# Chunked attention, gated convolution and two projections on one core: another written-out order, which places GpSimd's pieces beside VectorE pieces that read PSUM or one operand

## The chip, the cores and the metric

One core of a Trainium2 chip runs the whole kernel as one program. The metric is device time in microseconds (us), as the median of several runs; smaller is better. The engines are TensorE (PE in the profile, its weight loads PEld), VectorE (DVE), ScalarE (ACT), GpSimd (POOL) and SyncE (SP), which issues the DMAs here.

## What is computed

Attention within chunks of 64 positions, for 8 batches, 8 heads, 576 positions and 64 values per head, and behind it a block in which a causal convolution of five taps makes a gate for a projection. Inputs and outputs are 32-bit floats.

```python
scores = scale * np.matmul(q_c, k_c.transpose(0, 1, 2, 4, 3))
attn = np.exp(scores - np.max(scores, axis=-1, keepdims=True))
attn = attn / (np.sum(attn, axis=-1, keepdims=True) + 1e-09)
x = np.matmul(attn, v_c)            # heads side by side: batch x 576 x 512
for k in range(K):                  # K = 5, zeros ahead of each batch
    gate_pre += conv_w[k] * xp[:, k:k + S, :]
out = (1 / (1 + np.exp(-gate_pre)) * (x @ w_val)) @ w_out
```

## The kernel before, in words

The 8 x 576 positions are cut into nine stages g = 0 to 8 of 512 positions each. The features lie on the partitions, 128 at a time, so a stage has four feature blocks and two pairs of them, p = 0 and 1.

The order of all work is written out by hand, or by a planner, in the string `ORDER`. It is a list of short pieces; the loop at the end of the function calls one Python function for each, in that order, and `tc.keep_in_program_order` keeps it. Every engine works through its own pieces strictly in that order, and waits where a piece needs the result of another engine or a buffer that is still in use. Which buffer a piece gets is written out too, in `SLOTS`: one digit for each allocation of a name.

The pieces, with the engine that does each:

- `lq`, `lk`, `lv g p`: loads of queries, keys and values (SyncE; tiles `qt`, `kt`, `vt`, two buffers each). `lw n c`: block c of the weights of `x @ w_val` (n = v) or of the output projection (n = o); `lc`: the tap weights. The raw weights go into `acc` buffers. `st g t`: store of an output tile `o`.
- `w1` to `w9`, `wa`, `wb`: each weight block arrives as raw bits and is split into a high part (`v_hi`, `o_hi`) and a low part (`v_lo`, `o_lo`). `w1`, `w3`, `w4`, `w7` are VectorE's, `w2`, `w5`, `w6` ScalarE's, `w8`, `wa`, `wb` GpSimd's; with a D behind the name (`waD`) VectorE does the piece.
- Attention of a pair: `S g p b` (score products into PSUM tile `s`, 32 recorded products each), `mx` (row maximum), `sb` (subtract it, into `e_row`), `ex` (exponential, ScalarE), `sm` (row sum `rs` and its reciprocal), `nm` (normalise, tile `en`; GpSimd, or VectorE as `nmD`), `T` (eight transposes into `et`), `ec` (copy to `eb`, ScalarE), `A` (products with the values, into two `ps` banks of PSUM).
- The projection's input: `xr` (rounded copy `xh`, ScalarE), `xd` (the rest, `xl`, VectorE, which reads PSUM), `xc` (plain copy `x` for the convolution), `hl` (the four positions ahead of a stage, GpSimd).
- Convolution of feature block h: `k0` (first tap, ScalarE, or VectorE as `k0D`), `k g h j` (taps j = 1 to 4, VectorE, SCALAR_TENSOR_TENSOR on `acc`), `sg` (sigmoid, ScalarE).
- Value projection: `V g m c`, three products of 512 columns (`xh` with `v_hi`, `xh` with `v_lo`, `xl` with `v_hi`) added into one of four `ps` banks over c = 0 to 3; `gm g m` multiplies that bank by the gate (VectorE, tile `gt`) and frees it.
- Output projection: `gr` (rounded copy `gh`, ScalarE), `gd` (the rest, `gl`, GpSimd, or VectorE as `gdD`), `P g t c` (three products again, into a `ps` bank), `oc` (copy to `o`, ScalarE, or VectorE as `ocD`).
- `W n`: n products of a zero tile `warm`, whose result is used by nobody. `zr`, `zi`, `zw` set constants.

Pieces of several stages stand mixed. At the start the four `v` and four `o` weight blocks are split between the softmax work of the first pairs and the first taps, all largely on VectorE. The four `ps` banks serve `A`, `V`, `P` and `W` in turn, so a `V` or `P` piece with c = 0 waits until VectorE or ScalarE has read the bank's last contents.

A line number of the profile is of little use here, since every instruction is recorded on the one line of `run`; the tile names tell the pieces apart.

Of the kernel before, what the change touches and what calls it, by code (L numbers as in the profile page):

```python
# [514 lines left out]
```

## Time and profile before

| | |
|---|---|
| median of 3 runs | 305.24 us (304.71 to 305.42) |
| the profiled execution's own time | 305.96 us |
| its span, first to last instruction | 304.2 us |
| TensorE busy / VectorE busy | 274.9 us / 266.1 us |
| ScalarE busy / GpSimd busy | 185.2 us / 85.5 us |
| moved by DMA | 42.47 MB |

Busy time is the union of an engine's instructions, waits inside them included: a VectorE instruction that is held by another engine counts as busy and shows a longer duration. Products are pipelined, so a product's own duration (0.40 us) is longer than the distance from one start to the next. The timeline merges neighbours of one kind, with their count behind x.

### The profile page before, as it was taken

To read this page: it belongs to the slowest core of one execution; us is meant where nothing else is said; L and a number is where in the kernel's file an instruction comes from. 1 tells how busy PE (TensorE), PEld (TensorE's weight loads), DVE (VectorE), ACT (ScalarE), POOL (GpSimd) and SP (SyncE) were. 2 spreads that over 40 slices of the span, in tenths; PEclk is the share of its full clock that TensorE was granted. 3 is DMA by queue.
4 is the path that set the end of the run, shared out by engine and by line. 5 is a ranking of instruction groups with operands and counts; after the bars stand their busy time and mean duration, and the time that the engine had idled before them with its cause. 6 is when DMAs were issued, how large, how long until landed. Compare 5 with 4: busy or idle time off the path is not lost.

```text
span 304.2 us, 7897 instructions
## 1 busy us (share of the span) xinstructions
PE 274.9 (90%) x3356; PEld 218.4 (72%) x3361; DVE 266.1 (87%) x374; ACT 185.2 (61%) x314; POOL 85.5 (28%) x77
## 2 busy tenths in 40 slices
PE   0688663989999999999899989999999999999995
PEld 0456442768887888888777877887888888788883
DVE  4799999989999999999999999979998877679710
ACT  4268656676678796885816976465567825732401
POOL 1535740424155026106430541063200600100100
PEclk9999996999999999999999999999999999999999
DMA  6997403601481752362662732124250014211013
GB/s 239 414 404 246 155 2 125 214 11 43 166 284 65 276 183 102 105 224 91 209 237 110 236 113 71 69 90 155 102 213 36 1 45 124 78 71 50 19 76 132
DMA packets 14291, 42.47 MB, mean 140 GB/s; under 512 B 1712, under 2 KB 1712, under 8 KB 14256
## 3 DMA queue, kind: packets, MB, share of 16 engines
q1 hardware_dynamic: 14256, 41.97, 38.6%
q8 instruction: 26, 0.43, 0.6%
q14 instruction: 9, 0.07, 0.1%
HBM read 32.53 MB, written 9.44 MB: 138 GB/s over the span
## 4 chain that ended last, share of the span: by engine, by line
PE 57%; DVE 31%; DMA 5%; issue 4%; SPq 1%; ACT 1%; DVEq 0%; ACTq 0%
PE ps L160 50%; DVE acc L160 12%; PE s L160 4%; DVE gt L160 4%; DVE e_row L160 4%; DVE rs L160 3%; DVE mx L160 3%; DVE xl L160 2%; DMA kt<-in_k 2%; PE et L160 2%; DMA vt<-in_v 2%; DVE gate L160 1%; SPq L160 1%; DVE gl L160 0%; DVE v_lo L160 0%
## 5 line engine op out<-in xcount | busy, mean ns | idle before, releaser
L160 DVE SCALAR_TENSOR_TENSOR acc<-x,cw,acc 128x516 f32<-128x516 f32 (+1 forms) x144 | 113.1, 818 | 2.9 <-ACT acc L160 1.8
L160 POOL TENSOR_TENSOR gl<-gt,gh 128x512 fp32r<-128x512 f32 x24 | 32.7, 1365 | 149.5 <-ACT gh L160 149.5
L160 PE MATMUL ps<-xh,v_hi 128*128 128x512 f32 x144 | 59.5, 413 | 6.2 <-DVE xl L160 6.2
L160 PE MATMUL ps<-xl,v_hi 128*128 128x512 f32 x144 | 57.3, 398 | 3.1 <-DVE xl L160 3.1
L160 PE MATMUL ps<-o_hi,gh 128*128 128x512 f32 x144 | 58.4, 405 | 0.0
L160 PE MATMUL ps<-xh,v_lo 128*128 128x512 f32 x144 | 57.2, 397 | 0.0
L160 PE MATMUL ps<-o_lo,gh 128*128 128x512 f32 x144 | 56.9, 395 | 0.0
L160 PE MATMUL ps<-o_hi,gl 128*128 128x512 f32 x144 | 56.9, 395 | 0.0
L160 ACT ACTIVATE gate<-acc 128x512 f32<-128x512 uint32 (+8 forms) x72 | 30.3, 466 | 20.9 <-DVE acc L160 20.7
L160 POOL TENSOR_TENSOR en<-e_row,rs 128x1024 f32<-128x1024 f32 x16 | 32.4, 2022 | 23.0 <-DVE rs L160 22.5
L160 PEld LDWEIGHTS ps<-xh,v_hi 128*128 128x128 f32 x144 | 27.2, 189 | 13.1 <-DVE xl L160 6.6
L160 ACT COPY o<-ps 128x512 f32<-128x512 f32 x27 | 15.7, 584 | 32.1 <-PE ps L160 30.3
L160 PEld LDWEIGHTS ps<-xl,v_hi 128*128 128x128 f32 x144 | 27.2, 189 | 10.4 <-DVE xl L160 3.9
L160 PE MATMUL s<-kt,qt 64*64 64x64 f32 x1152 | 23.5, 231 | 12.3 <-DMA kt<-in_k 10.1
L160 PEld LDWEIGHTS s<-kt,qt 64*64 64x64 f32 x1152 | 20.8, 144 | 17.1 <-issue 15.5
L160 PEld LDWEIGHTS ps<-o_hi,gl 128*128 128x128 f32 x144 | 27.1, 188 | 6.5
L160 PEld LDWEIGHTS ps<-o_hi,gh 128*128 128x128 f32 x144 | 27.1, 188 | 6.5 <-issue 0.2
L160 PEld LDWEIGHTS ps<-xh,v_lo 128*128 128x128 f32 x144 | 27.4, 190 | 5.5
L160 PEld LDWEIGHTS ps<-o_lo,gh 128*128 128x128 f32 x144 | 27.1, 188 | 5.8
L160 ACT CAST gh<-gt 128x512 fp32r<-128x512 f32 x36 | 22.1, 618 | 13.7 <-DVE gt L160 13.5
L160 ACT ACTIVATE e_row<-e_row 128x1024 f32<-128x1024 f32 x18 | 19.1, 1061 | 17.8 <-DVE e_row L160 17.7
L160 ACT CAST xh<-ps 128x512 fp32r<-128x512 f32 x36 | 20.8, 592 | 14.8 <-PE ps L160 14.3
(56 smaller groups left out, 373.6 us busy)
## 6 DMA issues: line engine op xcount, KB each, us to landing
qt<-in_q SPq DMA_DIRECT2D x18, 512.0 KB, 4.9
kt<-in_k SPq DMA_DIRECT2D x18, 512.0 KB, 6.4
vt<-in_v SPq DMA_DIRECT2D x18, 512.0 KB, 4.5
out<-o SPq DMA_DIRECT2D x36, 256.0 KB, 2.3
acc<-in_moe_w_val SPq DMA_DIRECT2D x4, 512.0 KB, 6.3
acc<-in_moe_w_out SPq DMA_DIRECT2D x4, 512.0 KB, 9.0
raw_cw<-in_moe_conv_w SPq DMA_DIRECT2D x1, 20.0 KB, 1.7
```

The costliest lines, as they stand in the source:

```text
L160: return tc.keep_in_program_order(fn(*args, **kwargs))
```

## The change

`ORDER` and the strings of `SLOTS` that go with it are replaced as a whole; no function, no shape and no tile size differs. What the new list has otherwise than the old one, counted piece by piece:

- the same computation, but other engines for some pieces: four more `gd` on VectorE (16 for 12), two more `nm` on VectorE (4 for 2), two more `oc` on VectorE (11 for 9), one `xc` fewer on VectorE (4 for 5); four first taps fewer on VectorE (1 for 5); of the weight pieces `wb v 1`, `wb v 2`, `wb o 0`, `wb o 3`, `wa o 0` and `w8 o 3` go from VectorE to GpSimd, and `wa v 0`, `wa v 2` and `w8 o 2` from GpSimd to VectorE;
- 87 warm products in eight pieces `W` for 49 in six; `W 8` and `W 16` now stand ahead of the first score products;
- everything else in another order, on all engines and on SyncE's queue.

```diff
--- before.py
+++ after.py
-ORDER = """zw,zr 1,lc,hl 0,zi,lw v 1,zr 0,lw v 0,lq 0 0,lk 0 0,lw v 2,lw v 3,w3 c 0,w1 c 0,lk 0 1,w2 c 0,w5 c 0,w4 c 0,lq 0 1,
-w7 c 0,w8D c 0,w9,w1 v 1,w3 v 1,w2 v 1,w5 v 1,w1 v 0,w4 v 1,lw o 2,w2 v 0,lv 0 0,w3 v 0,w5 v 0,w7 v 1,w6 v 1,w4 v 0,
-lw o 0,w8D v 1,w6 v 0,S 0 0 0,w7 v 0,S 0 0 1,waD v 1,W 14,w8 v 0,mx 0 0,lq 1 0,lk 1 0,wa v 0,sb 0 0,w3 v 2,ex 0 0,
-w3 v 3,wbD v 1,w5 v 2,w1 v 2,S 0 1 0,sm 0 0,wb v 0,S 0 1 1,W 10,lk 1 1,w1 v 3,lv 0 1,mx 0 1,nm 0 0,w2 v 3,lq 1 1,
...
+ORDER = """zw,hl 0,lc,zi,lw v 1,W 8,zr 1,zr 0,lw v 0,lq 0 0,lk 0 0,lw v 2,lk 0 1,w1 c 0,w3 c 0,w2 c 0,lw v 3,w5 c 0,w4 c 0,
+w7 c 0,lq 0 1,W 16,w1 v 1,w3 v 1,w2 v 1,w8D c 0,w9,w1 v 0,w5 v 0,w4 v 1,w2 v 0,w3 v 0,w5 v 1,w7 v 1,w6 v 1,w4 v 0,
+w8D v 1,w6 v 0,S 0 0 0,w7 v 0,S 0 0 1,waD v 1,W 14,w8 v 0,w5 v 2,mx 0 0,lk 1 0,lw o 2,lq 1 1,wb v 1,sb 0 0,w1 v 2,
+ex 0 0,w1 v 3,w3 v 2,waD v 0,w2 v 2,S 0 1 0,w2 v 3,sm 0 0,wb v 0,S 0 1 1,w5 v 3,W 9,lq 1 0,mx 0 1,lv 0 0,nm 0 0,
+lw o 0,lk 1 1,sb 0 1,lv 1 0,T 0 0,w4 v 2,ex 0 1,W 7,w3 v 3,w7 v 2,w6 v 2,sm 0 1,w8 v 2,ec 0 0,A 0 0,w4 v 3,nmD 0 1,
+S 1 0 0,xr 0 0 0,lv 0 1,S 1 0 1,w7 v 3,xc 0 0 1,lw o 1,T 0 1,w1 o 0,xc 0 0 0,lk 2 0,waD v 2,w5 o 0,W 11,mx 1 0,
+wb v 2,w2 o 0,ec 0 1,xd 0 0 0,w8 v 3,k0 0 0,sb 1 0,w3 o 0,ex 1 0,S 1 1 0,k 0 0 1,lw o 3,S 1 1 1,lq 2 0,w4 o 0,
...
-    acc="01230132130213021302132013",
-    qt="010101101000110010",
-    kt="010101010010101110",
-    gate="0123450123450134343013250413250143201543021534201543",
-    gt="01010101101010101010010110100110101101011001",
-    vt="010101010101101001",
+    acc="01231032013201320132013210",
+    qt="010110100001001101",
+    kt="010101010100010101",
+    gate="0123450312450312451403241503241053241032451023405123",
+    gt="01010110100110101010101010011001101010101010",
+    vt="010010110100001010",
...
```

Three places, as the built programs have them. First GpSimd, from `nm 1 0` on (tile `en`; `gate`, `o_hi` and `o_lo` belong to weight pieces `w8`, `wa`, `wb`; `gl` to `gd`). Before:

```order
L160 TENSOR_TENSOR en_543<-e_row_63,rs_439 128x1024
L160 TENSOR_TENSOR gate_522<-gate_522,gate_346 128x512
L160 TENSOR_TENSOR en_575<-e_row_64,rs_547 128x1024
L160 TENSOR_TENSOR gate_633<-gate_633,gate_626 128x512
L160 TENSOR_TENSOR gate_626<-gt_623,o_hi 128x512
L160 TENSOR_TENSOR gl_795<-gt_753,gh_755 128x512
```

and now:

```order
L160 TENSOR_TENSOR en_569<-e_row_63,rs_550 128x1024
L160 TENSOR_TENSOR gate_407<-gt_439,o_hi 128x512
L160 TENSOR_TENSOR o_lo<-gate_407,gate_413 128x512
L160 TENSOR_TENSOR en_633<-e_row_64,rs_578 128x1024
L160 TENSOR_TENSOR gate_649<-gate_649,gate_612 128x512
L160 TENSOR_TENSOR gate_612<-gt_731,o_hi 128x512
```

Before, `nm 1 0` and `nm 1 1` have one weight piece (`w8 o 2`) between them; now two, `wa o 0` and `wb o 0`.

VectorE at the same place, from the row sum of pair 1 1 on (`acc<-x,cw,acc` is a tap; `gt<-acc`, `gate<-acc`, `gt<-gate,gt` and `gate<-gt` are `w3`, `w1`, `w4` and `w7`). Before:

```order
L160 TENSOR_REDUCE rs_547<-e_row_64 128x16
L160 RECIPROCAL rs_547<-rs_547 128x16
L160 SCALAR_TENSOR_TENSOR acc_545<-x_74,cw,acc_545 128x512
L160 SCALAR_TENSOR_TENSOR acc_437<-x_74,cw,acc_437 128x512 x2
L160 SCALAR_TENSOR_TENSOR acc_545<-x_74,cw,acc_545 128x512
L160 TENSOR_TENSOR gate_348<-gt_406,o_hi 128x512
L160 SCALAR_TENSOR_TENSOR acc_437<-x_74,cw,acc_437 128x512 x2
L160 TENSOR_SCALAR gt_623<-acc_397 128x512
```

and now:

```order
L160 TENSOR_REDUCE rs_578<-e_row_64 128x16
L160 RECIPROCAL rs_578<-rs_578 128x16
L160 SCALAR_TENSOR_TENSOR acc_436<-x_71,cw,acc_436 128x512
L160 TENSOR_SCALAR gt_593<-acc_211 128x512
L160 TENSOR_SCALAR gate_612<-acc_396 128x512
L160 SCALAR_TENSOR_TENSOR gt_593<-gate_518,gt_593 128x512
L160 SCALAR_TENSOR_TENSOR acc_436<-x_71,cw,acc_436 128x512
L160 TENSOR_SCALAR gate_518<-gt_593 128x512
L160 SCALAR_TENSOR_TENSOR acc_436<-x_71,cw,acc_436 128x512 x2
```

Before, five taps and the two steps `waD` and, later, `wbD` of block o 0 follow the row sum; now one tap, then `w3 o 2`, `w1 o 1` and `w4 o 2`, and the other taps behind them.

SyncE's queue, where the last loads of the first stages stand (`acc<-in_moe_w_out` is `lw o`, and the first `vt` is `lv 1 1`). Before:

```order
L160 DMA acc_397<-in_moe_w_out 128x1024
L160 DMA qt_464<-in_q 128x1024
L160 DMA acc_637<-in_moe_w_out 128x1024
L160 DMA kt_641<-in_k 128x1024
L160 DMA qt_691<-in_q 128x1024
L160 DMA kt_694<-in_k 128x1024
L160 DMA vt_705<-in_v 128x1024
```

and now:

```order
L160 DMA acc_460<-in_moe_w_out 128x1024
L160 DMA qt_478<-in_q 128x1024
L160 DMA kt_516<-in_k 128x1024
L160 DMA vt_545<-in_v 128x1024
L160 DMA qt_548<-in_q 128x1024
L160 DMA qt_641<-in_q 128x1024
L160 DMA qt_875<-in_q 128x1024
```

Before, `lv 1 1` is behind `lq 3 0` and `lk 3 0`, which need the buffers of `lq 2 0` and `lk 2 0`; now it is ahead of `lq 2 1`, `lq 4 1` and `lq 3 0`.

## Rows read from the trace of the kernel before

**Rows 1.** The page's first part: engine, busy us (share of the span), instructions.
```profile
PE 274.9 (90%) x3356; PEld 218.4 (72%) x3361; DVE 266.1 (87%) x374; ACT 185.2 (61%) x314; POOL 85.5 (28%) x77
```

**Rows 2.** Chain that ended last, in order of time: start us, us, what.
```profile
9.94 2.02 PE s L160 x64
...
55.45 6.58 DMA vt<-in_v
...
233.46 0.93 PE s L160 x64
...
258.66 41.89 PE ps L160 x238
```

**Rows 3.** Timeline of TensorE: start us, us, engine, line, operation, out<-in, count, [idle before].
```profile
12.27 3.50 PE L160 MATMUL ps<-warm 128*128 128x512 bf16 x13 [0.33 <-issue]
...
50.38 0.79 PE L160 MATMUL ps<-xh,v_hi 128*128 128x512 f32 x1 [6.20 <-DVE xl L160]
...
56.44 0.39 PE L160 MATMUL ps<-xh,v_hi 128*128 128x512 f32 x1
...
58.53 0.39 PE L160 MATMUL ps<-xh,v_hi 128*128 128x512 f32 x1
...
62.17 1.16 PE L160 MATMUL ps<-eb,vt 64*64 64x64 f32 x64 [1.38 <-DMA vt<-in_v]
...
176.13 0.69 PE L160 MATMUL s<-kt,qt 64*64 64x64 f32 x32 [1.08 <-DVE acc L160]
```

**Rows 4.** Windows: stretch, its us, PE, PEld, DVE, ACT, POOL busy, PEclk, DMA.
```profile
60.00:70.00 10.00, 8.62 (x154) 6.49 (x153) 8.98 (x14) 7.62 (x14) 2.50 (x2) 1.00 0.06 21
...
90.00:100.00 10.00, 9.77 (x161) 7.84 (x160) 9.96 (x14) 8.20 (x14) 4.62 (x5) 1.00 0.26 102
...
140.00:150.00 10.00, 9.22 (x163) 7.56 (x162) 9.93 (x13) 8.10 (x13) 5.05 (x4) 1.00 0.45 146
...
160.00:170.00 10.00, 9.56 (x169) 7.79 (x168) 9.86 (x14) 7.80 (x14) 2.45 (x2) 1.00 0.25 84
170.00:180.00 10.00, 8.92 (x160) 7.25 (x159) 9.97 (x13) 8.20 (x17) 3.06 (x3) 1.00 0.68 230
```

**Rows 5.** Timeline of GpSimd.
```profile
26.60 2.50 POOL L160 TENSOR_TENSOR gate<-gt,v_hi 128x512 f32<-128x512 f32 x2
32.44 1.32 POOL L160 TENSOR_TENSOR gate<-gate,gate 128x512 f32<-128x512 f32 x1 [3.34 <-DVE gate L160]
...
40.49 2.17 POOL L160 TENSOR_TENSOR en<-e_row,rs 128x1024 f32<-128x1024 f32 x1 [0.77 <-DVE rs L160]
```

**Rows 6.** Timeline of VectorE.
```profile
28.00 1.38 DVE L160 TENSOR_SCALAR gt<-acc 128x512 uint32<-128x512 uint32 x1
...
32.21 0.41 DVE L160 TENSOR_SCALAR gt<-acc 128x512 uint32<-128x512 uint32 x1
...
33.14 1.22 DVE L160 TENSOR_REDUCE mx<-s 128x16 f32<-128x1024 f32 x1
34.27 1.29 DVE L160 SCALAR_TENSOR_TENSOR gt<-gate,gt 128x512 uint32<-128x512 uint32 x1
...
40.24 4.29 DVE L160 SCALAR_TENSOR_TENSOR acc<-x,cw,acc 128x512 f32<-128x512 f32 x4
...
54.43 1.77 DVE L160 SCALAR_TENSOR_TENSOR acc<-x,cw,acc 128x512 f32<-128x512 f32 x1
56.13 0.68 DVE L160 TENSOR_TENSOR gt<-ps,gate 128x512 f32<-128x512 f32 x1
56.73 1.21 DVE L160 TENSOR_REDUCE mx<-s 128x16 f32<-128x1024 f32 x1
...
74.63 6.75 DVE L160 SCALAR_TENSOR_TENSOR acc<-x,cw,acc 128x516 f32<-128x516 f32 x10
```

**Rows 7.** Windows again, one of one microsecond.
```profile
48.00:49.00 1.00, 0.00 (x0) 0.00 (x0) 1.00 (x3) 1.00 (x3) 0.00 (x0) 0.50 0.00 0
```

More of the change, by code (lines that the diff above doesn't have):

```diff
@@ new lines @@
+k0 2 1,k 1 3 4,V 1 2 3,gr 1 1,xd 2 0 0,T 2 1,sg 1 3,gd 1 1,gm 1 2,V 1 3 2,xd 2 0 1,gr 1 2,V 1 3 3,sb 3 0,ec 2 1,
+gd 1 2,P 1 3 0,P 1 3 1,gm 1 3,k 2 1 1,P 1 3 2,ex 3 0,k 2 1 2,A 2 1,k 2 0 1,gr 1 3,S 3 1 0,xc 2 1 0,sm 3 0,gd 1 3,
+S 3 1 1,xr 2 1 0,P 1 0 0,lk 5 1,xr 2 1 1,lq 4 0,P 1 0 1,mx 3 1,nm 3 0,xc 2 1 1,lv 3 1,P 1 3 3,k0 2 2,xd 2 1 0,
+P 1 0 2,oc 1 3,sb 3 1,hl 3,P 1 0 3,k0 2 3,T 3 0,xd 2 1 1,ex 3 1,k 2 1 3,V 2 3 0,ec 3 0,k 2 3 1,V 2 3 1,k 2 0 2,
+V 2 3 2,oc 1 0,k 2 3 2,st 1 0,V 2 3 3,k 2 1 4,A 3 0,k 2 3 3,S 4 0 0,k 2 0 3,xr 3 0 0,S 4 0 1,xr 3 0 1,k 2 0 4,
@@ new lines @@
+P 3 0 3,k 4 1 4,P 3 1 0,k 4 3 1,P 3 1 1,sg 4 1,k 4 3 2,V 4 0 0,oc 3 0,k 4 3 3,st 3 0,V 4 0 1,k 4 3 4,V 4 0 2,
+k 4 2 3,sg 4 3,V 4 0 3,k 4 2 4,P 3 1 2,k 4 0 4,P 3 1 3,gm 4 3,sg 4 0,S 6 1 0,sm 6 0,oc 3 1,A 5 1,S 6 1 1,gm 4 0,
+xr 5 1 0,lv 5 0,nm 6 0,V 4 2 0,mx 6 1,lk 7 1,gr 4 0,V 4 2 1,lq 7 1,xr 5 1 1,st 3 1,V 4 2 2,xc 5 1 0,sb 6 1,gd 4 0,
+ec 5 0,V 4 2 3,xcD 5 1 1,V 4 1 0,gr 4 3,xd 5 1 0,sg 4 2,V 4 1 1,gd 4 3,xd 5 1 1,k0 5 2,V 4 1 2,gm 4 2,A 5 0,k0D 5 3,
+k 5 3 1,S 7 0 0,ex 6 1,lv 6 1,V 4 1 3,k 5 3 2,xr 5 0 0,T 6 0,k 5 3 3,xr 5 0 1,P 2 2 0,gm 4 1,ec 6 0,P 2 2 1,
@@ new lines @@
+k 5 1 2,V 5 1 0,k 6 0 2,oc 2 0,gm 5 0,V 5 2 0,sg 5 2,k 5 1 3,V 5 2 1,gr 5 0,k 5 1 4,A 6 1,sm 7 0,gd 5 0,sg 5 1,
+S 7 1 0,S 7 1 1,gr 5 3,xc 6 1 0,V 5 2 2,gd 5 3,mx 7 1,lq 8 0,xc 6 1 1,lv 7 0,V 5 1 1,st 4 0,V 5 1 2,hl 7,sb 7 1,
+lk 8 1,xr 6 1 0,nm 7 0,V 5 1 3,lv 7 1,xr 6 1 1,xd 6 1 0,V 5 2 3,k0 6 2,xd 6 1 1,P 4 2 0,k0 6 3,gm 5 1,P 4 1 0,
+gm 5 2,T 7 0,k 6 3 1,P 4 2 1,ex 7 1,P 4 2 2,ec 7 0,sm 7 1,P 4 2 3,gr 5 2,A 7 0,ocD 4 2,gd 5 2,S 8 1 0,st 4 2,
+xc 7 0 0,xcD 7 0 1,S 8 1 1,gr 5 1,V 6 3 0,xr 7 0 0,gd 5 1,V 6 3 1,xr 7 0 1,xd 7 0 0,V 6 3 2,k0 7 0,xd 7 0 1,nm 7 1,
@@ new lines @@
+hl 8,P 6 3 1,xr 7 1 0,P 6 3 2,oc 4 1,xd 7 1 0,P 6 3 3,xr 7 1 1,st 4 1,k0 7 3,V 7 3 0,xd 7 1 1,V 7 3 1,sb 8 0,
+V 7 3 2,k 7 0 2,ex 8 0,V 7 3 3,k 7 1 3,P 5 1 0,ex 8 1,k 7 1 4,P 5 1 1,k 7 0 3,P 5 1 2,k 7 0 4,P 5 1 3,k 7 3 1,
+P 5 0 0,oc 5 1,sm 8 0,P 5 0 1,st 5 1,P 5 0 2,V 7 0 0,nmD 8 0,sg 7 0,V 7 0 1,oc 6 3,k 7 3 2,V 7 0 2,st 6 3,lv 8 0,
+k 7 3 3,V 7 0 3,P 5 0 3,k 7 3 4,V 7 2 0,gm 7 0,ocD 5 0,V 7 2 1,gr 7 0,k 7 2 1,sg 7 3,V 7 2 2,gdD 7 0,sg 7 1,V 7 2 3,
+k 7 2 2,T 8 0,k 7 2 3,P 6 0 0,ec 8 0,k 7 2 4,P 6 0 1,gm 7 3,sg 7 2,P 6 0 2,P 6 0 3,gm 7 2,A 8 0,sm 8 1,gr 7 2,
@@ new lines @@
+sg 8 0,k 8 3 2,sg 8 2,P 6 1 2,k 8 3 3,P 6 1 3,V 8 0 3,k 8 3 4,oc 6 1,V 8 1 3,sg 8 3,st 6 1,gm 8 0,V 8 2 0,gm 8 1,
+gr 8 0,V 8 2 1,gdD 8 0,gr 8 1,V 8 2 2,gdD 8 1,V 8 2 3,gm 8 3,P 8 3 0,gm 8 2,gr 8 3,P 7 0 0,gr 8 2,P 7 0 1,gdD 8 2,
+P 8 3 1,gdD 8 3,P 8 3 2,P 8 3 3,P 8 0 0,ocD 8 3,P 8 0 1,st 8 3,P 8 0 2,P 7 1 0,P 7 0 2,P 7 0 3,P 8 1 0,oc 7 0,
+P 7 1 1,st 7 0,P 7 1 2,P 8 2 0,P 7 1 3,P 8 1 1,oc 7 1,P 8 2 1,st 7 1,P 8 2 2,P 8 2 3,P 8 0 3,ocD 8 2,P 8 1 2,st 8 2,
+ocD 8 0,P 7 2 0,st 8 0,P 8 1 3,P 7 2 1,P 7 2 2,ocD 8 1,P 7 2 3,st 8 1,oc 7 2,st 7 2"""
@@ L96 @@
 SLOTS = dict(
     x="010101010",
-    acc="01230132130213021302132013",
-    qt="010101101000110010",
-    kt="010101010010101110",
-    gate="0123450123450134343013250413250143201543021534201543",
-    gt="01010101101010101010010110100110101101011001",
-    vt="010101010101101001",
+    acc="01231032013201320132013210",
+    ps="012320122300211321301320123012310213023201320320120102132012031203120323021320201321312321302123"
+       "21032310231003120310",
+    qt="010110100001001101",
+    kt="010101010100010101",
@@ L114 @@
     xl="012012012012021021",
-    gh="012345670132456745671032567402316745",
-    gl="012345670123456745671023564703214765",
-    o="010110111110100110000110111001011010",
+    gh="012345670231456745670312467502136574",
+    gl="012345670132456745670321476501237564",
+    o="010110001001111010111010100101010101",
 )
```

120 lines of the change are left out of this document (45 added, 75 removed).

## Prediction

> **What bounds the kernel now.** Read the engine table first [rows 1]: TensorE is busy for 274.9 us of 304.2 and VectorE for 266.1. Neither is far from full, so the table does not say which of them sets the end; the chain that ended last does, followed backwards [rows 2]. Its last 41.89 us, from 258.66 us on, are nothing but TensorE, 238 instructions without a gap; behind them stand one copy and one store. Two older pieces of it matter as much: the first score products at 9.94 us, which wait for the first keys, and the wait for a load of values that was issued at 55.45 us. The rest up to 176 us alternates between VectorE and TensorE.
>
> Next look at how TensorE runs once it has work [rows 3]. From 56.44 to 58.53 us it starts nine 512-column products, 0.232 us each, so a piece of three takes 0.70 us. At 50.38 us it starts again after 6.20 us of idling for VectorE's `xl`. **The end is therefore the restart near 50 us, plus the work still left, plus the waits after it.** The ten-microsecond windows give those later waits as what TensorE's busy time lacks of 10.00 [rows 4]: 1.38 + 0.23 + 0.78 + 0.44 + 1.08 = 3.9 us, and every other such window from 70 us on is full up to 300 us. Before the restart the idle time is larger but it belongs to the first 50 us, where VectorE prepares weights, does the softmax of the first pairs and the first taps, and is never idle for long.
>
> Last, what GpSimd does to VectorE [rows 5, 6]. A weight step of 0.41 us (at 32.21) takes 1.38 us at 28.00, beside the second of two GpSimd subtractions (26.60, 2.50 us for two); four taps from 40.24 us take 4.29 us, beside `en` at 40.49; ten free taps in a row take 6.75 us, 0.675 each. The maximum at 33.14 us, which reads PSUM alone, takes 1.22 us although GpSimd works on `gate` from 32.44 us, and the one at 56.73, 1.21 us.
>
> **The change, part by part.**
>
> *Earlier warm matmuls.* W 8 and W 16 now run while the first keys are still on their way. At 9.94 us the first 64 score products take 2.02 us; the same 64 take 0.93 us at 233.46 us [rows 2]. If TensorE is at its higher level by then, VectorE's first maximum starts 1.0 us sooner. The 24 extra matmuls cost at most 24 x 0.27 = 6.5 us (13 recorded in 3.50 us at 12.27, slow ones among them [rows 3]), inside the 9.94 us of waiting, hence nothing. If they all went at half the rate of a 512-column product, 2 x 0.232 x 24 = 11.1 us, the scores would start up to 2 us late but run fast, net 1 us later than now. I take -1.0, since the 3.50 us row is the same instruction; ends -1.1 and +1.0.
>
> *VectorE's queue up to the first gate product (`gm 0 0`, 56.13 us).* The order shows 62 instructions from the first maximum to it before and 60 now. Gone from this stretch: one tap (0.675), one `xd`, `wb v 1`, `wb v 2`, `wa o 0`, `wb o 0`; new in it: `wa v 0`, `wa v 2`, `w8 o 2`, `wb o 2`. At 0.60 us for each two-input step (the start of one at 56.13 to the next start, 56.73 [rows 6]) this is -0.675 - 5 x 0.60 + 4 x 0.60 = **-1.3 us**.
>
> *Contention in that stretch.* Before: 1.38 - 0.41 = 0.97 (28.00), 1.29 - 0.68 = 0.61 (34.27, less a two-input step of the same size, 56.13), 4.29 - 2.70 = 1.59 (40.24, less four free taps), 1.70 - 0.675 = 1.03 (54.43 to the next start); together **4.2 us**. Now: GpSimd's `w8`, `wa`, `wb` of the value weights fall beside maxima, row sums, `xd` and score subtractions, as the change says, and cost nothing there (33.14). But its queue then holds `en`, `wa o 0`, `wb o 0` and `en` of the next pair in a row, and VectorE's holds, after the row sum of pair 1 1, a tap, `w3 o 2`, `w1 o 1`, `w4 o 2`. Laid end to end with the durations above, `wa o 0` ends 0.3 us after that tap wants to start; then a 1.25 us piece stands in front of `w3 o 2` and a 1.9 us piece (2.17 at 40.49, less its own wait) in front of `w1 o 1`. I estimate 0.3 + 1.0 + 1.9 = **3.2 us**, so the change does not clear this stretch. Ends: 0, if the three pieces slip under the row sum, and 0.3 + 1.25 x 2 + 1.9 + 2 x 1.25 = 7.2, if `w8 o 1` and `wa o 1` also land on taps.
>
> What no row here shows is `w1` (one input, two steps apart in memory) beside a GpSimd piece; `w3`, its neighbour, was held (28.00). The Trainium skill's page "SBUF — State Buffer", section "Who interferes with whom", says that GpSimd and a VectorE instruction with two SBUF inputs, or one in a two-port mode, exclude each other for a whole instruction. By that `w1 o 1` waits in full; if it ran free, `w4 o 2` behind it would wait instead and the stretch would be 0.3 us shorter.
>
> So `gm 0 0` starts at 56.13 - 1.0 - 1.3 - 4.2 + 3.2 = 52.8 us and ends 0.68 us later. In the new order it is what frees the PSUM bank for TensorE's next piece, `V 0 2 0`: restart at **53.5 us, 3.1 us later** than 50.38.
>
> *Work done by then.* Before the restart TensorE has finished seven `V` pieces of stage 0; now eight, also the score products of pair 2 0 (0.93) and the transposes of pair 1 1, eight of 128 columns, which by their columns are two products, 0.5, and with switching up to 0.9 (estimate from rows 3). 0.70 + 0.93 + 0.8 = **-2.4 us** of remaining work. TensorE idles about as long as now before the restart (some 7 us against 6.20), so its clock falls as it does at 48 us, where the granted clock is 0.50, the 1.2 GHz level [rows 7], and the slow first products cost the same.
>
> *Waits after the restart.* 1.38 us at 62.17 is the load of `vt` issued at 55.45, because it stood on SyncE behind two loads that wait for score products of pair 2 0; it now stands ahead of them and lands long before its use: gone. 1.08 us at 176.13 [rows 3] is put down to a tap, but scores need no tap; keys for that pair are a likelier cause, and they are now issued farther ahead. The remaining 1.45 us are VectorE being late. With the new order I laid VectorE's running sum (queue and steps of 0.60, 0.675 and, for maxima and the like, 1.13 us, 33.14 to 34.27) against TensorE's 0.70 us pieces: VectorE is 0 to 1 us ahead from 53 to 62 us and 4 to 6 us ahead from 95 to 130 us. Then 2 to 3 us of new contention would still be covered. I keep 1.0 us of waits for chances such as a late `eb` copy or an output slot: **-3.9 + 1.0 = -2.9 us**; ends -3.9 and 0.
>
> *The rest.* VectorE gets four more `gl` and two more `en` (4 x 0.60 + 2 x 1.13) and gives four first taps to ScalarE: about +1 us in all with the copies, all after 56 us, covered by the lead above; without it, 1 us. The other 14 extra warm matmuls (W 18 instead of W 13 and so on) stand where TensorE waits for `xl`; uncovered they would cost 0.22 us each. `vt` and one weight load now stand on SyncE behind a query load that waits for the scores of pair 0 1; they land about 1 us before their use: 0, at worst +1.
>
> **Sum:** +3.1 - 2.4 - 2.9 = **-2.2 us** on the span of 304.2, so 302.0. The profiled execution took 305.96 us, the median of the runs is 305.24; taken off the median, **303.0 us**.
>
> **Rivals.**
>
> 1. *GpSimd's three pieces slip past.* If the `en`, `wa o 0`, `wb o 0` run sits under the row sum and one `xd` more, its 3.2 us fall to about 0.7. For it: the chain in front of them hangs on one ScalarE copy that may come sooner. Against it: `en` alone takes 1.9. Price -2.5 more: 300.5 us.
>
> 2. *The change does not do what it says after the restart.* The contention merely moves, VectorE stays the bound up to 176 us, and of the 3.9 us only the 1.38 us of the load goes; the 1 us more that VectorE gets is then uncovered. The sum is +3.1 - 2.4 - 1.4 + 1.0 = +0.3: 305.5 us, no change that can be told. For it: VectorE lacks less than 0.2 us in every window of rows 4 but the first, and the new order gives it more to do. Against: its lead above.
>
> 3. *The weight stretch gets worse.* All five GpSimd pieces from `wa o 0` to `wa o 1` stand in front of two-input or weight steps, 7.2 instead of 3.2 us: restart at 57.5 us, sum +1.8, 307 us. It decides when `gm 0 0` starts later than 52.8 + 2.2 + 0.6 = 55.6 us. For it: at 40.24 and 54.43 exactly such neighbours were caught, and GpSimd's queue has no pause there now. Against: `w8 o 1` and `wa o 1` have a gate product, `xd` and a maximum beside them. The Trainium skill's page "SBUF — State Buffer", in the same section, says that whichever of the two starts first keeps the shared port for its whole instruction, which speaks for this rival; the tap at 54.43, held for 1.03 us, agrees.
>
> **How the numbers follow.** Forecast 0.46, rival 1 0.20, rival 2 0.17, rival 3 0.17. A measurement of this kernel can tell about 0.2%, 0.6 us, from no change: faster is below 304.6. The forecast and rival 1 lie there, with small parts at their edge: faster 0.66, same 0.17, slower 0.17. The range takes the forecast's own ends, most of rival 1 and of rival 2: 299.8 to 306.0 us; left out are the best of rival 1 and the worst of rival 3.
>
> **What would show it.** Right: the first 64 score products take about 1 us; `gm 0 0` starts between 52 and 54 us; TensorE's wait for `vt` near 62 us is gone; its windows from 60 us on lack about 1 us in all; taps and weight steps of over 1 us stand between 36 and 42 us and hardly elsewhere. Wrong: `gm 0 0` after 55.6 us, or TensorE windows after 60 us that still lack 3 us or more, or the slow score products at the start still there.

## The result, and the profile after

The changed kernel takes **301.84 us** (301.51 to 301.96) against 304.98 for the kernel before in the same series: ratio 0.9887, 95% interval 0.9856 to 0.9919, 3.1 us less. The forecast was 303.0 us, 2.2 us less, with a range of 299.8 to 306.0. The profiled execution took 301.91 us with a span of 300.0.

Against [rows 1] TensorE is now busy 7 us longer in a shorter span (24 more warm matmuls ahead of the first scores are most of it), VectorE 8 us less, with one instruction fewer. The first part of the page:

```profile
PE 282.0 (94%) x3394; PEld 222.1 (74%) x3399; DVE 258.1 (86%) x373; ACT 187.1 (62%) x318; POOL 77.0 (26%) x74
```

TensorE's timeline, to be held against [rows 3]: the first scores, the restart, and the attention product that had waited for the load of values. The first line is the scores before, in the same view; the others are now.

```profile
9.94 1.99 PE L160 MATMUL s<-kt,qt 64*64 64x64 f32 x64 [9.94 <-DMA kt<-in_k]
...
9.55 1.16 PE L160 MATMUL s<-kt,qt 64*64 64x64 f32 x64 [1.54 <-DMA kt<-in_k]
...
53.12 0.79 PE L160 MATMUL ps<-xh,v_hi 128*128 128x512 f32 x1 [6.89 <-DVE gt L160]
60.09 1.16 PE L160 MATMUL ps<-eb,vt 64*64 64x64 f32 x64
```

The scores take 1.16 us instead of 1.99. The restart is at 53.12 us and waits for `gt`, the first gate product, as laid out. The wait of 1.38 us for `vt` is gone. TensorE's waits from 50 us on (engine and line, what it waited for, us in total, times, longest), first of the kernel before:

```profile
PE ps L160 <- DVE xl L160: 6.2, 1, 6.2
PE ps L160 <- DMA vt<-in_v: 1.4, 1, 1.4
PE s L160 <- DVE acc L160: 1.1, 1, 1.1
PE ps L160 <- ACT eb L160: 0.8, 1, 0.8
PE et L160 <- ACT eb L160: 0.4, 1, 0.4
PE s L160 <- DVE e_row L160: 0.2, 1, 0.2
```

and of the changed kernel:

```profile
PE ps L160 <- DVE gt L160: 6.9, 1, 6.9
PE s L160 <- issue: 0.2, 1, 0.2
```

Apart from the restart, 3.9 us of waits have become 0.2. The windows of [rows 4] that lacked something are full:

```profile
60.00:70.00 10.00, 10.00 (x163) 8.36 (x163) 9.80 (x17) 8.43 (x14) 2.80 (x2) 1.00 0.55 210
...
170.00:180.00 10.00, 10.00 (x226) 8.19 (x225) 9.39 (x15) 8.56 (x15) 3.74 (x5) 1.00 0.56 181
```

Not all of it is gain. After the restart TensorE stays longer at its lower level than before (the third number from the end of such a row is the granted clock: 0.50 is 1.2 GHz):

```profile
53.00:54.00 1.00, 0.88 (x2) 0.78 (x3) 1.00 (x3) 0.90 (x2) 0.92 (x2) 0.50 0.00 0
...
58.00:59.00 1.00, 1.00 (x4) 0.81 (x3) 0.00 (x0) 0.00 (x0) 0.00 (x0) 0.60 0.00 0
```

Now the weight stretch. GpSimd's queue, then VectorE's beside it:

```profile
33.31 1.91 POOL L160 TENSOR_TENSOR en<-e_row,rs 128x1024 f32<-128x1024 f32 x1
35.18 1.30 POOL L160 TENSOR_TENSOR gate<-gt,o_hi 128x512 f32<-128x512 f32 x1
36.56 1.61 POOL L160 TENSOR_TENSOR o_lo<-gate,gate 128x512 fp32r<-128x512 f32 x1
38.13 2.09 POOL L160 TENSOR_TENSOR en<-e_row,rs 128x1024 f32<-128x1024 f32 x1
```

```profile
34.78 1.23 DVE L160 TENSOR_REDUCE rs<-e_row 128x16 f32<-128x1040 f32 x1
...
36.22 0.81 DVE L160 SCALAR_TENSOR_TENSOR acc<-x,cw,acc 128x512 f32<-128x512 f32 x1
36.95 1.50 DVE L160 TENSOR_SCALAR gt<-acc 128x512 uint32<-128x512 uint32 x1
38.37 2.12 DVE L160 TENSOR_SCALAR gate<-acc 128x512 f32<-128x512 f32 x1
```

The row sum at 34.78 runs at its full speed beside GpSimd; the tap loses 0.07 us, `w3 o 2` 1.08 (1.50 against the 0.42 of a free one), `w1 o 1` 1.70 (2.12 against 0.42), 2.9 us together. Both steps have one operand and were held all the same, so the "one operand" of the title holds for the row sum and not for them. Summed over all VectorE pieces that last over 0.1 us longer than the free ones of their kind (0.76 us a tap, 0.70 a step with two inputs, 0.43 with one, 1.25 the maxima, sums and the like), the holds come to 3.2 us, where they were 13.8 before. Where did the other 10.6 go? VectorE's own waits from 56 to 230 us, before and after, show it. Before:

```profile
DVE x L160 <- PE ps L160: 1.6, 1, 1.6
DVE xl L160 <- ACT x L160: 0.6, 1, 0.6
DVE xl L160 <- ACT xh L160: 0.5, 2, 0.3
```

After:

```profile
DVE gt L160 <- PE ps L160: 3.7, 5, 2.4
DVE mx L160 <- PE s L160: 2.3, 3, 1.0
DVE xl L160 <- ACT x L160: 1.5, 3, 0.7
```

With the smaller lines, 3.5 us have become 10.7: most of what VectorE gained it now spends waiting, above all for TensorE, 2.4 us of it at 57 us, behind the slow products of the restart.

### The profile page after: what moved, and what is told of

Its sections match the earlier page's. It is cut to its first block, busy times and chain, and to the rows that moved or that the text cites. A ratio compares the mean times of both kernels' runs of the same rounds, so it can differ in the third digit from the quotient of the medians.

```text
span 300.0 us, 7975 instructions
## 1 busy us (share of the span) xinstructions
PE 282.0 (94%) x3394; PEld 222.1 (74%) x3399; DVE 258.1 (86%) x373; ACT 187.1 (62%) x318; POOL 77.0 (26%) x74
## 4 chain that ended last, share of the span: by engine, by line
PE 82%; DVE 7%; DMA 7%; SPq 1%; issue 1%; ACT 0%; DVEq 0%
PE ps L160 73%; PE s L160 5%; PE et L160 4%; DMA qt<-in_q 3%; DVE acc L160 2%; DMA vt<-in_v 2%; DVE gate L160 2%; SPq L160 1%; DMA acc<-in_moe_w_out 1%; DVE gt L160 1%; DVE rs L160 1%; DVE xl L160 1%; DVE mx L160 0%; DVE o_lo L160 0%; ACT o L160 0%
## 5 line engine op out<-in xcount | busy, mean ns | idle before, releaser
L160 DVE SCALAR_TENSOR_TENSOR acc<-x,cw,acc 128x516 f32<-128x516 f32 (+1 forms) x144 | 103.3, 753 | 1.9 <-ACT acc L160 0.5
L160 PE MATMUL ps<-o_hi,gh 128*128 128x512 f32 x144 | 58.6, 407 | 0.0
L160 PE MATMUL ps<-xh,v_lo 128*128 128x512 f32 x144 | 57.9, 402 | 0.0
L160 POOL TENSOR_TENSOR gl<-gt,gh 128x512 fp32r<-128x512 f32 x20 | 25.8, 1292 | 87.4 <-ACT gh L160 87.3
L160 ACT COPY o<-ps 128x512 f32<-128x512 f32 x25 | 14.6, 583 | 40.5 <-PE ps L160 38.0
L160 POOL TENSOR_TENSOR en<-e_row,rs 128x1024 f32<-128x1024 f32 x14 | 27.4, 1960 | 17.1 <-DVE rs L160 17.1
L160 DVE TENSOR_TENSOR gt<-ps,gate 128x512 f32<-128x512 f32 x36 | 24.3, 681 | 7.1 <-PE ps L160 5.3
L160 ACT ACTIVATE acc<-x,cw 128x516 f32<-128x516 f32 (+1 forms) x35 | 24.6, 728 | 4.0 <-DVE gt L160 3.8
L160 ACT CAST xh<-ps 128x512 fp32r<-128x512 f32 x36 | 20.5, 594 | 10.6 <-PE ps L160 10.6
L160 DVE TENSOR_TENSOR xl<-ps,xh 128x512 fp32r<-128x512 f32 x36 | 23.9, 682 | 2.9 <-ACT x L160 1.5
```

The source lines that it names most:

```text
L160: return tc.keep_in_program_order(fn(*args, **kwargs))
```

## The experiments

Theory: the end is TensorE's restart near 50 us plus its work plus its waits, so it counts when VectorE reaches the restart, at which clock TensorE then runs, and which VectorE piece is late behind it. Rivals: VectorE's own queue sets the pace whatever TensorE does; or loads, not held taps, made the waits. Each run has its own runs of the kernel before beside it, so ratios are compared.

**1 and 2: parts of the change made in the kernel before.** First the load of values alone, ahead of the two loads that it stood behind; then also five `en` pieces on VectorE.

```diff
-S 2 0 1,k 0 3 4,V 0 0 3,lq 3 0,k 0 0 4,lk 3 0,T 1 1,lv 1 1,w7 o 1
+S 2 0 1,k 0 3 4,V 0 0 3,lv 1 1,lq 3 0,k 0 0 4,lk 3 0,T 1 1,w7 o 1
...
-nm 4 0 ... nm 4 1 ... nm 5 1 ... nm 6 0 ... nm 6 1
+nmD 4 0 ... nmD 4 1 ... nmD 5 1 ... nmD 6 0 ... nmD 6 1
```

> Kernel before with one piece moved: lv 1 1 is issued on SyncE ahead of lq 3 0 instead of behind it and lk 3 0. Theory (the end is TensorE's restart plus its work plus its waits): the wait of 1.38 us at 62.17 us goes and nothing takes its place, about 304.0 us, 1.0 to 1.4 below the kernel before. Rival (after the restart VectorE sets the pace, a TensorE that comes earlier only waits later): TensorE's waits after 70 us grow by as much, no change, 304.7 to 305.3 us.

> As the first, and besides the five en pieces that held a VectorE tap after 110 us (pairs 4 0, 4 1, 5 1, 6 0, 6 1) are done by VectorE itself, at 1.13 us each. They held their taps for 7.2 us together (excess over 0.76), so VectorE gains 7.2 - 5.7 = 1.5 us. Theory (TensorE's waits at 143.9, 164.1 and 174.2 us, 2.7 us together, come from held taps): the waits shrink by about 1.5 us, 1.5 us below the first kernel, about 302.5 us. Rival (these waits are loads of keys, or VectorE's own amount of work): as the first kernel within 0.4 us, the waits stay.

Measured: 304.42 us, ratio 0.9974 (0.9957 to 0.9991), and 303.77 us, 0.9953 (0.9934 to 0.9972), against 305.22. The load alone is worth 0.8 us of its 1.4 (by the interval 0.3 to 1.3). Waits of TensorE from 50 us on in the first of the two:

```profile
PE ps L164 <- DVE xl L164: 4.8, 1, 4.8
PE s L164 <- DMA kt<-in_k: 1.5, 2, 0.9
PE ps L164 <- ACT eb L164: 0.8, 1, 0.8
PE et L164 <- ACT eb L164: 0.5, 1, 0.5
PE ps L164 <- DVE gt L164: 0.3, 1, 0.3
```

Without the restart 3.1 us are left of 3.9: the 1.4 us are gone, and 0.6 have come back in the others. With the five `en` on VectorE as well the same lines add up to 1.8 us, so in the trace 1.3 of the 1.5 us of VectorE do reach TensorE. In the time the second run stands 0.65 us below the first, and their intervals overlap: the direction fits, the size isn't shown.

**3: the changed kernel without its first warm matmuls.**

```diff
-zi,lw v 1,W 8,zr 1
+zi,lw v 1,zr 1
-lq 0 1,W 16,w1 v 1
+lq 0 1,w1 v 1
-    ps="012320122...
+    ps="2320122...
```

> Changed kernel without W 8 and W 16. Theory: the first 64 score products take about 2.0 us instead of 1.2, the first maximum starts 1 us later, with it the first gate product and the restart, and no later wait absorbs it: about 303.0 us, 1.0 to 1.3 above the changed kernel. Rival (the weight stretch waits for ScalarE, GpSimd or a load anyway, or VectorE's 2.4 us of idling at 57 us takes it up): within 0.3 us of the changed kernel.

302.51 us, ratio 0.9897 (0.9871 to 0.9924): 0.7 us above the change, and by the time alone not told apart from it. The trace is clearer. The 64 scores take 1.98 us again, and VectorE has a wait that it did not have. TensorE's timeline, then VectorE's waits from 15 to 60 us:

```profile
8.68 1.98 PE L164 MATMUL s<-kt,qt 64*64 64x64 f32 x64 [8.68 <-DMA kt<-in_k]
```

```profile
DVE gate L164 <- DMA acc<-in_moe_w_out: 1.2, 1, 1.2
DVE mx L164 <- PE s L164: 0.6, 1, 0.6
```

The slow scores, and the slow warm matmuls behind them (14 in 5.04 us, where the changed kernel has 13 recorded in 2.97), delay the second scores, a query load that SyncE issues behind those, and with it the block of output weights behind that (issued at 18.53 instead of 16.88 us). So the first gate product comes 1.85 us later (54.24 against 52.39), though the keys landed 0.87 us sooner here. The warm start thus brings loads forward too, which the forecast did not have; that the time moved by less goes with a shorter slow stretch after the later restart (the granted clock rises near 58.6 us in both).

**4: one held step less in front of the restart.**

```diff
-w4 o 2,S 2 0 1,nm 1 1,k0 0 3
+w4 o 2,S 2 0 1,nmD 1 1,k0 0 3
```

> Changed kernel with en of pair 1 1 done by VectorE (1.13 us) instead of GpSimd, where it held w1 o 1 for 1.7 us at 38.37 us. Theory (a held step in front of the restart costs its time in full): the first gate product starts 0.6 us earlier, restart 52.5 us, about 301.2 us. Rival 1 (w1 is not slowed by GpSimd but by something else): gate product 1.1 us later, about 303.0 us. Rival 2 (after the restart TensorE is then held by VectorE): restart earlier, time unchanged.

300.76 us, ratio 0.9848 (0.9825 to 0.9872). VectorE's timeline:

```profile
36.55 1.51 DVE L164 TENSOR_SCALAR gt<-acc 128x512 uint32<-128x512 uint32 x1
37.98 0.41 DVE L164 TENSOR_SCALAR gate<-acc 128x512 f32<-128x512 f32 x1
```

`w1 o 1` is free (0.41), so it was GpSimd's `en` that held it; `w3 o 2` is held as before, by `wb o 0`. From the held stretch to the first gate product VectorE gains 0.56 us (0.98 us earlier there, 0.42 of it already ahead of the stretch), as expected; the 1.1 us between the medians is more than that, and within what the two intervals allow.

**5: the old neighbourhood put back at three places** behind the row sums of pairs 3 0, 5 1 and 6 1.

```diff
-sm 3 0, ... mx 3 1, ... xd 2 1 1, ... k 2 1 3, ... k 2 0 2
+sm 3 0,k 2 1 3,k 2 0 2, ... mx 3 1, ... xd 2 1 1
-sm 5 1, ... xd 4 1 0, ... mx 6 0, ... k 4 1 2, ... k 4 1 3
+sm 5 1,k 4 1 2,k 4 1 3, ... xd 4 1 0, ... mx 6 0
-sm 6 1, ... xd 6 0 0, ... mx 7 0, ... k 5 3 4, ... k 5 2 1
+sm 6 1,k 5 3 4,k 5 2 1, ... xd 6 0 0, ... mx 7 0
```

> Changed kernel with the neighbourhood undone at three places: behind the row sums of pairs 3 0, 5 1 and 6 1 (93, 146 and 176 us) two taps stand again before VectorE's next PSUM piece, beside the en that GpSimd starts there; all else is as in the changed kernel. In the kernel before such a tap was held 1.4 us, so 3 x 1.4 = 4.2 us more for VectorE. Theory as predicted (VectorE is 4 to 6 us ahead there, so 2 to 3 us of contention are covered): 301.8 to 302.4 us. Rival (the trace of the changed kernel shows results only 0.4 to 1.4 us old where TensorE takes them, so each held tap costs what is over that): 0.6 to 1.0 us each, 303.6 to 304.8 us.

308.11 us, ratio 1.0097 (1.0065 to 1.0129): 6.3 us slower than the change, slower even than the kernel before. Both expectations fall. GpSimd's `en` and VectorE's two taps at the first place, then TensorE's waits from 90 to 210 us:

```profile
93.28 2.17 POOL L164 TENSOR_TENSOR en<-e_row,rs 128x1024 f32<-128x1024 f32 x1 [0.25 <-DVE rs L164]
```

```profile
93.03 2.98 DVE L164 SCALAR_TENSOR_TENSOR acc<-x,cw,acc 128x516 f32<-128x516 f32 x2
```

```profile
PE ps L164 <- DVE xl L164: 3.2, 2, 2.7
PE ps L164 <- DVE gl L164: 1.6, 1, 1.6
```

Two taps take 2.98 instead of 1.42 us, and the `xd` and maxima behind them come late by the taps and the hold. At the second place two `en` run one after the other and hold both taps (by 0.48 and 1.52 us). This run mixes two things, the holds and the moved taps (1.34 us each time); the next pair takes them apart.

**9 and 10: extra GpSimd work of one size, once beside taps, once beside PSUM pieces and reductions,** VectorE's order untouched. The pieces of the two runs read different tiles, as the code shows.

```diff
+    dum = const.tile([P, 2, T], F32, name="dum")
+    def beside(src, g, i):
+        if src == "x":
+            one, two = xl[g, i].bitcast(F32), xh[g, i].bitcast(F32)
+        else:
+            one = two = acc[g, i][:, i % 2, begin(g) - HALO:][:, :T].unsqueeze(1).broadcast_to([P, 2, T])
+        run(G.tensor_tensor, out=dum, in0=one, in1=two, op=ALU.subtract)
...
-xd 2 1 1, ... xd 3 1 1, ... xd 4 0 1, ... xd 6 0 1
+xd 2 1 1,Z x 2 1, ... xd 3 1 1,Z x 3 1, ... xd 4 0 1,Z x 4 0, ... xd 6 0 1,Z x 6 0
```

In the second kernel `Z a 3 1`, `Z a 4 0`, `Z a 5 3`, `Z a 6 3` stand behind `k 3 1 4`, `k 4 0 4`, `k 5 3 3`, `k 6 3 1` instead.

> Changed kernel, VectorE's order untouched, with four extra GpSimd subtractions of 1024 columns (their result is not used), each started by an xd (2 1 1, 3 1 1, 4 0 1, 6 0 1) so that it runs beside the row of taps behind it, at 98, 123, 132 and 184 us. Each should hold a tap 1.65 us, as en did. Theory as predicted (a lead of 4 to 6 us from 95 to 130): 301.8 to 302.2 us. Rival 1 (the cover is VectorE's own pauses plus how old its results are when TensorE takes them, 0.4 to 1.5 us at each place): 0.2 to 0.8 us each, 303.0 to 304.2 us. Rival 2 (no cover at all): 4 x 1.65, 308 us.

> The same four extra GpSimd subtractions, each started by a tap (3 1 4, 4 0 4, 5 3 3, 6 3 1) behind which VectorE's next pieces read PSUM or one operand (134, 162, 174 and 203 us). Theory of the change (such pieces are not held): VectorE's maxima, row sums and gate products keep their durations, 301.6 to 302.2 us. Rival (GpSimd's time itself counts: its own gd and en come 2 us later and are waited for): 302.5 to 304.0 us with VectorE's durations unchanged.

Beside taps: **307.26 us**, ratio 1.0069 (1.0043 to 1.0096). Beside PSUM pieces: **301.44 us**, 0.9898 (0.9865 to 0.9932), the time of the change. The two taps behind the first `xd` of the former (one operation of a line: count, ns least/median/greatest, first and last start):

```profile
L164 DVE SCALAR_TENSOR_TENSOR acc<-x,cw,acc x2: 747/1822/2897, 97.7 to 98.3; 128x516 f32<-128x516 f32 x2
```

The latter: its four extra pieces in the groups of GpSimd (busy us, mean ns, idle before), and VectorE beside the first of them (134 us):

```profile
L164 POOL TENSOR_TENSOR dum<-acc 128x1024 f32<-128x1024 f32 x4 | 7.6, 1894 | 31.8 <-DVE acc L164 31.8
```

```profile
133.56 1.22 DVE L164 TENSOR_REDUCE mx<-s 128x16 f32<-128x1024 f32 x1
134.69 0.68 DVE L164 TENSOR_TENSOR gt<-ps,gate 128x512 f32<-128x512 f32 x1
135.29 1.21 DVE L164 TENSOR_TENSOR e_row<-s,mx 128x1024 f32<-128x1024 f32 x1
```

Maximum, gate product and score subtraction keep 1.22, 0.68 and 1.21 us, and laid beside the changed kernel VectorE's lead of 0.4 us before the first extra piece is still 0.3 us after the last. In the ninth run a tap goes from 0.75 to about 2.90 us, four times, 8.6 us in all, of which 5.4 reach the end: each place covers some 0.8 us on average, not 2 to 3. (A fifth tap, at 200.56 us, then meets a `gl` and takes 1.87 us; what it lost is made up again by 204 us.) The time lies outside the ranges of the theory and of rival 1, and 0.7 us under that of rival 2. The holds were 2.15 us each and not the 1.65 expected; with 2.15, the cover of rival 1 (0.4 to 1.5 us a place) gives 2.6 to 7.0 us more, which takes in the 5.4. Laid beside the changed kernel, VectorE of the ninth run is 0.2 us ahead before the first place, 1.2 us late before the second, 2.5 before the third, 4.0 before the fourth, and 6.1 after it. The Trainium skill's page "SBUF — State Buffer", section "Who interferes with whom", says that a VectorE instruction with two SBUF inputs contends with a GpSimd one that reads SBUF, that a reduction never does, and that the later of the two is blocked in full; by that rule the tap waits and the maximum doesn't, and the trace agrees (2.90 and 1.22 us).

**6 and 11: the price of the cold restart.** Warm matmuls into the PSUM tile of the transposes, where TensorE idles; in the second run `wb o 0` on VectorE too.

```diff
+    def keep_warm_et(n):
+        ps = tile_of("et", [P, 8, P], F32, banks)[:, 0:4, :].rearrange("p a b -> p (a b)")
+        for _ in range(n):
+            run(E.matmul, ps, lhsT=warm[:, :P], rhs=warm, start=True, stop=True)
...
-nm 1 1, ... A 1 0,waD o 2,T 1 1
+nmD 1 1, ... A 1 0,waD o 2,X 24,T 1 1
...
-wb o 0,w3 o 2
+wbD o 0,w3 o 2
```

> Changed kernel with en of pair 1 1 on VectorE (as in the fourth run) and 24 more warm matmuls, written into the PSUM tile of the transposes, ahead of the transposes of pair 1 1, where TensorE idles from 46 us to its restart. Theory (the restart's products at 1.28 instead of 0.70 us are the price of the idling, 2.7 us in all, and the first gate products wait for them 2.4 us): granted clock 1.00 at the restart, V products 0.70 us from the first, 298.8 to 299.8 us against 300.76 of the fourth run. Rival (VectorE's pieces behind the restart are late as it is; TensorE then waits for the gate products): V products fast but a new wait before 65 us, 300.3 to 300.9 us.

> The sixth run (en 1 1 on VectorE, 24 warm matmuls ahead of the restart) and wb o 0 on VectorE too, 0.60 us, where it held w3 o 2 for 1.08 us. Theory (a held step before the restart costs its time): 0.5 us below the sixth run's 298.98 us, about 298.5. Rival (in front of the restart loads or ScalarE set the pace by now): same as the sixth run within 0.3 us.

298.98 us, ratio 0.9794 (0.9758 to 0.9830), and **297.58 us**, 0.9761 (0.9739 to 0.9782). TensorE in the second of them, with one window of it (the granted clock is the third number from the end):

```profile
44.24 5.35 PE L164 MATMUL et<-warm 128*128 128x512 bf16 x24
...
51.70 0.50 PE L164 MATMUL ps<-xh,v_hi 128*128 128x512 f32 x1 [0.96 <-DVE gt L164]
...
52.52 0.39 PE L164 MATMUL ps<-xh,v_hi 128*128 128x512 f32 x1
```

```profile
50.00:55.00 5.00, 4.04 (x21) 3.18 (x20) 5.00 (x8) 3.81 (x7) 4.39 (x4) 1.00 0.00 0
```

The next piece of three starts 0.82 us after the restart instead of 1.45, the granted clock is 1.00 from 40 to 70 us, and behind it no wait has come in its place. The sixth run's profile is of its slowest execution (300.81 us), which came to the restart only at 55.22 us, but its products run at the full rate there too (the next piece 0.80 us on). The ratio of the sixth run is 0.0054 below that of the fourth, 1.6 us; the two intervals just touch, and that of the eleventh lies clear of the fourth. With the traces, the theory of the cold restart holds, and its rival (VectorE late behind it anyway) falls. `wb o 0` gives another 0.0033 or 1.0 us, where 0.5 was expected; the intervals allow either, and nothing as well. The eleventh kernel is faster than both the kernel before (by 2.4%) and the change.

**7, 8 and 12: the first gate product earlier in VectorE's order.** The fourth run with that edit, with 14 warm matmuls (`X 14`) besides, and the eleventh run with a smaller move of the same kind.

```diff
-wbD o 2,w3 o 1,k 0 1 4,sg 0 0,w4 o 1, ... gm 0 0,w8 o 1,xd 1 0 0
+wbD o 2,w3 o 1,sg 0 0,gm 0 0,xd 1 0 0,k 0 1 4,w4 o 1, ... w8 o 1
...
-X 24,T 1 1,k 0 0 4,xr 1 0 0, ... k 0 1 4,sg 0 0,w4 o 1, ... gm 0 0
+X 20,T 1 1,k 0 0 4,sg 0 0,xr 1 0 0, ... k 0 1 4,gm 0 0,w4 o 1
```

> Changed kernel with en of pair 1 1 on VectorE, and the first gate product and xd 1 0 0 moved ahead of one tap, w4 o 1, another tap, w7 o 1 and a tap on VectorE. Theory (the restart waits for these two alone): restart 2.5 us earlier, and VectorE's 2.4 us of idling at 57 us shrinks as much: 298.4 to 299.6 us. Rival (VectorE's queue up to 75 us sets the pace, the order within it changes nothing): 300.4 to 301.2 us.

> Both: the early gate product of the seventh run and 14 warm matmuls ahead of the transposes of pair 1 1. If restart time and its clock both count, it gains over either alone, 297.5 to 298.8 us; if VectorE's queue is what is left, it equals the better of the two within 0.3 us, with TensorE waiting for gate products or for the bank of the second attention product between 55 and 65 us.

> The eleventh run with the first gate product 1.5 us earlier in VectorE's order, its sigmoid ahead of ScalarE's two copies that it stood behind, and 20 warm matmuls. In the seventh run the gate product waited 2.2 us for that sigmoid. Theory (a warm TensorE is bound by the restart alone, with results about 1 us old behind it): restart 1.5 us earlier, 0.5 to 1.2 us below the eleventh run. Rival (VectorE's queue to the second gate products is the bound once TensorE is warm): same as the eleventh run within 0.3 us, TensorE waiting near 57 us.

301.13 us, ratio 0.9871 (0.9836 to 0.9905); 299.78 us, 0.9830 (0.9793 to 0.9867); 298.03 us, 0.9784 (0.9752 to 0.9817). None is better than its neighbour without the move (the fourth, the sixth, which has more warm matmuls than the eighth, and the eleventh). In the seventh run the gate product waited for its sigmoid; VectorE, then ScalarE:

```profile
52.02 0.69 DVE L164 TENSOR_TENSOR gt<-ps,gate 128x512 f32<-128x512 f32 x1 [2.21 <-ACT gate L164]
```

```profile
48.91 0.59 ACT L164 CAST xh<-ps 128x512 fp32r<-128x512 f32 x1 [1.26 <-PE ps L164]
...
51.35 0.63 ACT L164 ACTIVATE gate<-acc 128x512 f32<-128x512 f32 x1
```

The sigmoid stands on ScalarE behind copies that wait for an attention product. In the twelfth run it stands ahead of them; then the first product comes at 50.45 us, and the next waits for `xl`, whose copies are now the later ones:

```profile
53.31 0.50 PE L164 MATMUL ps<-xh,v_hi 128*128 128x512 f32 x1 [1.90 <-DVE xl L164]
```

The wait has only moved: the second piece after the restart needs what the sigmoid was put in front of. In the eighth run, too, the restart is early (49.68 us) and fast, and TensorE then waits 1.7 us at 55.9 us for `eb`, the copy of the second attention product.

## Why the prediction was right, and where it was not

- **Earlier warm matmuls, -1.0.** The scores are 0.83 us shorter; the first maximum starts 1.22 us earlier, 0.39 of it because the keys landed earlier in this execution. Right in size. Missed was that loads behind the scores come forward too (run 3). The load of `vt` that was to land 1 us before its use came late: TensorE waited 1.00 us for it at 21.99 us. No wait of VectorE shows between 15 and 56 us, so at the restart no cost of it is seen.
- **The queue, -1.3, and contention, 4.2 to 3.2.** The first gate product was forecast at 52.8 us and came at 52.39, with the 0.39 us of the keys in it. Contention was 2.9 us, at the three pieces named (a tap, `w3 o 2`, `w1 o 1`), 36.2 to 40.5 us. Neither the first nor the third rival came about, and `w1`, for which no row stood, is held until GpSimd's piece ends (runs 4 and 11).
- **Restart at 53.5: 53.12.** Forecast +3.1 us, measured +2.7.
- **Work done by then, -2.4.** Right as counted: one product piece, two score pieces and one transpose fewer are left.
- **"The slow first products cost the same"** failed. The idling is 6.89 us against 6.20, the granted clock is at 0.50 from 49 to 58 us, and the slow pieces lose 2.7 us against 1.9 before: +0.8, and VectorE's wait of 2.4 us hangs on it. Runs 6 and 11 take this away.
- **Waits, 3.9 to 1.0, -2.9:** they went to 0.2, -3.7, so the second rival did not come about either. The load was priced at 1.4 and is worth 0.8 by itself (run 1), since other waits grow when TensorE comes earlier; only together with VectorE's earlier pieces does all of it go. The 1.1 us of scores at 176.13 us, put down to a tap, was a wait for keys, as the prediction guessed: a load of keys issued at 169.46 us lands at 176.00 us, and in run 1 the same scores wait 0.94 us for `kt` at 174.68 us.
- **"VectorE is 4 to 6 us ahead from 95 to 130 us; then 2 to 3 us of new contention would still be covered"** is the step that was wrong. It came from a running sum in which VectorE waits for nothing; but VectorE takes its operands from TensorE's last pieces and can't run ahead so far. In the changed kernel its results are often only 0.3 to 1.4 us old when TensorE takes them. That holds for 26 of the 55 times that TensorE, between 60 and 230 us, fills a PSUM bank that VectorE was the last to read. One of them, 0.4 us old, a gate product of VectorE and the first product into the bank that it freed:

```profile
106.78 0.69 DVE L160 TENSOR_TENSOR gt<-ps,gate 128x512 f32<-128x512 f32 x1 [0.22 <-PE ps L160]
107.89 0.39 PE L160 MATMUL ps<-xh,v_hi 128*128 128x512 f32 x1
```

In run 9, 8.6 us of holds from 98 to 189 us cost 5.4 us. The forecast survived because the new order left next to no contention there, not because there was cover. The added `gl` and `en` pieces, priced at about 1 us and called covered for the same reason, were not tried by themselves.

- **The sum.** In the profiled executions: +2.7 (restart) - 2.4 (work) - 3.7 (waits) + 0.8 (clock) = -2.6 of the -4.2 us of span. By the starts of TensorE's products, some 1.2 of the other 1.6 us lie in steps of about 0.1 us where it changes from one kind of product to another (131 changes from the restart on, for 140 before); the rest is spread thin. The forecast has no such term, and no run tested it. That the total came out as near as it did is in part luck: the clock (+0.8) and the further waits that went (-0.8) cancel. In the medians 3.1 us are left of the 4.2: the execution profiled before was 0.7 us above its median, the one after at its own.

What the change says of itself is so in part. The 13.8 us of held VectorE time became 3.2, and runs 9 and 10 show that extra GpSimd work costs 5.4 us beside taps and nothing beside PSUM pieces or reductions. Of what was gained after the restart, though, neighbours can account for 2.3 us of waits at most: 1.4 of the 3.7 were the load of values, and the 1.6 us above are no waits. Of the 2.3 us, 1.1 were that wait for keys, on which a held tap can only bear by delaying the load's issue. So the rival that loads made the waits is right for most of the 3.9 us. No run takes the neighbours alone out of the change (run 5 moves taps as well), so their share of the 3.1 us is not shown. That so little of the 10.6 us reaches the end is read from VectorE's waits: once no tap is held, TensorE is full from 60 us on and is the bound.

## What to carry to other kernels

Where VectorE and GpSimd work at the same time, put GpSimd's pieces beside VectorE pieces that read PSUM or reduce, and price the wrong neighbour at nearly GpSimd's whole duration (1.64 us of a tap for an `en` of 1.90). In this kernel two engines that feed each other had about as much cover as a result was old when it was taken, not what a running sum of one of them gave. Ahead of the point where TensorE starts for good, look first at what it did just before: keeping it busy through its idle stretch was worth more here (1.6 us) than any shift in the order of the pieces it waited for (runs 7, 8 and 12: nothing). When a piece is moved up, follow each operand through the queue of the engine that makes it.

## What the runs showed of the hardware that was not expected

- The hold goes both ways: an `en` that starts while a tap runs took 2.17 us (run 5, 93.28 us) against 1.90 to 1.91 beside maxima and `xd`, and the second tap lost 1.64 us. The tap that runs when GpSimd starts is not held (0.747 us in run 9), the one behind it is. The extra pieces of runs 9 and 10 (2.82 and 1.89 us) say nothing on this, since they read different tiles and no run has the former without taps.
- A VectorE step with a single, strided operand (`w1`) is held just as a tap: 2.12 against 0.41 us.
- After 6.9 us of idling TensorE stayed at the lower level (granted clock 0.50, 1.2 GHz) for more than 5 us of unbroken products; after 5.35 us of warm matmuls in the same place it started at the higher one (granted clock 1.00).
- The first scores, which wait for the first keys, start between 8.65 and 9.94 us in these executions of kernels that load the keys alike, which is 1.3 us of scatter ahead of all else.
